# A pooled-attention and gated-convolution kernel: fourteen held output pairs in place of eleven, and another place for the pooling of the next slot's second head pair

## Chip, cores, metric

One core of one Trainium2 chip. The metric is device time in microseconds (us), median over runs. Engines: PE is the matrix engine (PEld its weight loads), DVE the vector engine, ACT the scalar engine, POOL the engine that here issues most DMA transfers, SP one that issues a few. The granted clock is the share of its full clock that PE was given, 1.00 or 0.50 in these traces; 0.50 is called half clock.

## The reference, cut to what matters

```python
# q, k, v: (8, 8, 1152, 64) float32, small values (0.1 * randn)
q_pool = q.reshape(B, H, S // 2, 2, D).mean(axis=3)         # pairs of rows pooled
attn = softmax(q_pool @ k.T / sqrt(D))                      # per head
x = (attn @ v) as (B, S // 2, H * D)                        # (8, 576, 512)
gate = sigmoid(causal_conv5(x, conv_w))                     # per channel
out = ((gate * (x @ w_val)) @ w_out)                        # (8, 576, 512) float32
```

The kernel replaces the softmax by its first-order form, keeps a bound on the error, and computes exactly if the bound fails (it does not here). That part is not touched.

## The kernel before

32 pairs of heads in 16 slots of two (a = 2m, b = 2m + 1). In a slot PE sums k and v (`sm`) and forms the Gram matrices (`g`), ACT evacuates, PE applies them to the transposed pooled q (`xh`), and the convolution (`cps` on PE, three "taps" on DVE), the value matmuls (`vps`) and the gated value (`gv`, DVE) follow. The output matmuls (`ops`) of an earlier batch fill the gaps. Pooling q of the *next* slot (`pool_q`, DVE), its transposes (PE) and their evacuation (`mq`, ACT) are done in the slot before. `warm(n)` issues n idle matmuls (`wps`), whose result nobody reads. `moe` is true once a batch is ready for value and output matmuls (slot 2 on in even slots, slot 3 on in odd ones). Each engine runs its instructions in program order.

```python
NKV = 7            # pairs of inputs in flight
NOSB = 11          # SBUF buffers for finished outputs of two columns
...
def oevac(y, t0, m, ops, eng=None):
    osb = out_pool.tile([128, m, Dm], FP32, name="osb", tag=f"osb{m}", bufs=(3 if m == 1 else NOSB))
    if eng is None:
        nc.scalar.copy(out=osb, in_=ops[:, 0:m])
        held.append((y, t0, m, osb))     # stored only after the last load is issued
        return
    ...
# even slot
    gate(pb)
    gval(bt, 2, val(bt, 2, 0))
    norms(m - 1, g); stat(m, g)
    xhat(a, 1); xhat(b, 2); xevac(a); xevac(b)
    pool_q(a + 2)
    if moe:
        gval(bt, 3, val(bt, 3, 0))
    else:
        warm(3)
    transposes(a + 2)
    squares(m, g)
    conv(a, 1); conv(b, 2)
    tap(a, 0)
    pool_q(b + 2)
    tap(a, 1); tap(a, 2)
    if moe:
        ops = big("ops", 0)              # same PSUM bank as val(bt, 3, 0)
        outs(y, 512 * e, 2, ops, [0])
    ...
    transposes(b + 2)
    tap(b, 0)
    ...                                  # second half of outs, oevac
# odd slot
    ...
    if m + 1 < NSLOT:
        pool_q(a + 2)
        pool_q(b + 2)
    ...                                  # outs, oevac
    conv(a, 1); conv(b, 2, full=m + 1 == NSLOT)
    tap(a, 0)
    if m + 1 < NSLOT:
        transposes(a + 2)
    gate(pb)
    tap(a, 1); tap(a, 2)
    gval(bt, 0, val(bt, 0, 0))
    if m + 1 < NSLOT:
        transposes(b + 2)
    gate(a)
    gval(bt, 1, val(bt, 1, 1))
    if m + 1 < NSLOT:
        tap(b, 0)
    squares(m, g)
    if not moe:
        warm(22)                         # slot 1: idle matmuls
# end of each slot
while nload < min(NPAIR, a + NKV + 1):
    load_pair(nload); nload += 1
if nload == NPAIR:                       # from slot 12 on
    while held:
        store(*held.pop(0), nc.gpsimd)   # the same queue as the loads
```

## Time and profile before

| | before |
|---|---|
| time, median of three runs | 189.31 us (189.28 to 191.28) |
| the profiled run | 190.92 us, span 189.1 |
| PE, DVE, ACT busy | 162.4, 127.3, 111.0 us |
| loads running | to about 148 us (last issue at 136.75, and 11.3 to land) |
| slot 2 starts; slot 14 starts | 42.40; 154.33 us |

The span is the time from the first to the last instruction; the device time is some 1.8 us more. A slot's start, here and below, is its first `sm` matmul in the timeline. The profiled run is one of the longer ones. Besides the half clock at 32.1 to 38.9 us and at 151.6 to 155.0, it has one at 8.2 to 15.0 and one at the end. The views that carry the argument are in the prediction.

### The profile page before, as it was taken

The page shows a single profiled execution, that of the slowest core. Times are in us where ns is not written, and L with a number is a line of the kernel's source. Part 1 is how long each engine was busy: PE and PEld are TensorE (multiplying, and loading weights), DVE is VectorE, ACT ScalarE, POOL GpSimd, SP SyncE. Part 2 cuts the span into 40 slices and gives each one's busy share as a digit, 9 for nine tenths or more (in the row PEclk, how much of TensorE's full clock was granted, in tenths as well). Part 3 has the DMA queues.
Part 4 walks back from the last instruction along what each step waited for, and adds up shares of the span by engine and source line. Part 5 has one row for each costly group of instructions (what it writes and reads, how often), then busy time and mean ns, then how long its engine had stood idle before and what let it go on. Part 6 is the DMA issues. An engine that isn't in the chain of part 4 may idle for free.

```text
span 189.1 us, 5375 instructions
## 1 busy us (share of the span) xinstructions
PE 162.4 (86%) x2269; PEld 113.5 (60%) x2287; DVE 127.3 (67%) x236; ACT 111.0 (59%) x183; POOL 77.2 (41%) x122
## 2 busy tenths in 40 slices
PE   7367893899999999999999999999999599997920
PEld 2155562448678766876686767676867377665500
DVE  3216742906879895989798869888987547956550
ACT  2133952503869586877778686859687365865120
POOL 7945324544454454544344544454543351001000
PEclk9859998589999999999999999999999969999996
DMA  5999999999999999999999999999999999522061
GB/s 195 271 207 207 205 208 206 207 207 208 206 208 206 207 208 206 207 208 207 207 207 207 207 207 207 206 208 207 210 204 235 404 417 413 236 111 114 0 253 38
DMA packets 27864, 40.11 MB, mean 212 GB/s; under 512 B 1909, under 2 KB 24757, under 8 KB 27834
## 3 DMA queue, kind: packets, MB, share of 16 engines
q0 software_dynamic: 26624, 36.61, 97.9%
q1 hardware_dynamic: 938, 2.50, 3.8%
q10 hardware_dynamic: 272, 0.59, 0.9%
q8 instruction: 20, 0.33, 0.6%
q14 instruction: 10, 0.08, 0.1%
HBM read 58.73 MB, written 9.44 MB: 360 GB/s over the span
## 4 chain that ended last, share of the span: by engine, by line
PE 38%; DVE 28%; DMA 19%; ACT 4%; issue 3%; POOL 3%; DVEq 0%; POOLq 0%; ACTq 0%
PE ops L357 11%; DVE acc L318 9%; DVE gv L349 8%; PE vps L341 8%; DMA qn<-in_q_dram 7%; DVE acc L313 7%; DMA out_dram<-osb 6%; DMA kv<-in_k_dram 5%; PE sm L219 5%; PE g L229 4%; PE wps L414 3%; PE cps L303 2%; PE qt_ps L207 2%; PE xh L280 2%; DVE qp L198 2%
## 5 line engine op out<-in xcount | busy, mean ns | idle before, releaser
L318 DVE SCALAR_TENSOR_TENSOR acc<-x,convw_sb,acc 128x576 f32<-128x576 bf16 x62 | 50.5, 814 | 1.4
L341 PE MATMUL vps<-x,wval_sb 128*128 128x288 bf16 x256 | 38.6, 296 | 3.5 <-ACT osb L370 2.2
L357 PE MATMUL ops<-wout_sb,gv 128*128 128x512 bf16 x129 | 35.3, 379 | 0.8
L100 POOL DMA_DIRECT2D kv<-in_k_dram x31 | 22.2, 717 | 30.6 <-DMA kv<-in_v_dram 10.4
L349 DVE TENSOR_TENSOR gv<-vps,gate 128x576 bf16<-128x576 f32 x32 | 24.1, 755 | 12.3 <-PE vps L341 11.5
L313 DVE SCALAR_TENSOR_TENSOR acc<-x,convw_sb,cps 128x576 f32<-128x576 bf16 x31 | 25.1, 809 | 10.8 <-PE cps L303 10.8
L341 PEld LDWEIGHTS <-wval_sb 128*128 128x128 bf16 x256 | 24.5, 100 | 11.7 <-issue 5.0
L209 ACT COPY mq<-qt_ps 128x576 bf16<-128x576 bf16 x32 | 20.5, 639 | 18.4 <-PE qt_ps L207 17.4
L99 POOL DMA_DIRECT2D qn<-in_q_dram x31 | 20.0, 645 | 27.2 <-DVE acc L318 6.5
L287 ACT ACTIVATE x<-xh,stats 128x576 bf16<-128x576 f32 x32 | 22.0, 737 | 7.7 <-DVE stats L259 7.1
L102 POOL DMA_DIRECT2D kv<-in_v_dram x31 | 22.2, 716 | 9.4 <-DMA qn<-in_q_dram 7.0
L325 ACT ACTIVATE gate<-acc 128x576 bf16<-128x576 f32 x31 | 21.3, 686 | 5.3 <-DVE acc L318 5.3
L219 PE MATMUL sm<-kv,first 128*64 128x128 bf16 x576 | 20.4, 227 | 3.7 <-ACT kv L425 3.4
L219 PEld LDWEIGHTS <-first 128*64 128x64 bf16 x576 | 17.8, 114 | 9.2 <-issue 8.3
L265 ACT ACTIVATE mq<-g 64x128 bf16<-64x128 f32 x32 | 8.7, 272 | 23.0 <-PE g L245 22.8
L198 DVE TENSOR_TENSOR qp<-qn 96x768 bf16<-96x768 bf16 x31 | 16.5, 547 | 7.3 <-DMA qn<-in_q_dram 7.3
L370 ACT COPY osb<-ops 128x1024 f32<-128x1024 f32 (+1 forms) x17 | 15.9, 938 | 6.9 <-PE ops L357 4.0
L357 PEld LDWEIGHTS <-gv 128*128 128x128 bf16 x144 | 13.0, 98 | 11.2
L229 PE MATMUL g<-kv 128*64 128x128 bf16 x576 | 19.5, 222 | 0.0
L207 PE MATMUL qt_ps<-ident,qp 96*128 96x96 bf16 x192 | 14.3, 213 | 5.8 <-DVE qp L198 3.8
L364 POOL DMA_DIRECT2D out_dram<-osb x17 | 9.1, 537 | 24.1 <-ACT osb L370 13.6
L303 PE MATMUL cps<-x,diag 128*128 128x288 bf16 x128 | 18.9, 285 | 0.0
(68 smaller groups left out, 157.8 us busy)
## 6 DMA issues: line engine op xcount, KB each, us to landing
qn<-in_q_dram POOLq DMA_DIRECT2D x31, 288.0 KB, 10.9
kv<-in_k_dram POOLq DMA_DIRECT2D x31, 288.0 KB, 10.7
kv<-in_v_dram POOLq DMA_DIRECT2D x31, 288.0 KB, 11.3
out_dram<-osb POOLq DMA_DIRECT2D x14, 512.0 KB, 8.9
out_dram<-osb SPq DMA_DIRECT2D x2, 512.0 KB, 2.9
out_dram<-osb POOLq DMA_DIRECT2D x3, 256.0 KB, 8.2
k<-in_k_dram ACTq DMA_DIRECT2D x1, 576.0 KB, 4.8
q<-in_q_dram SPq DMA_DIRECT2D x2, 288.0 KB, 4.3
```

The lines of the kernel that those rows point to most:

```text
L100: nc.gpsimd.dma_start(out=t[:, W:2 * W].rearrange("p (h x) -> p h x", h=2), in_=k[b, h0:h0 + 2].rearrange("h (p t) d -> p h (t d)", p=128))
L102: nc.gpsimd.dma_start(out=t[:, 0:W].rearrange("p (h x) -> p h x", h=2), in_=v[b, h0:h0 + 2].rearrange("h (p t) d -> p h (t d)", p=128))
L219: nc.tensor.matmul(out=sms[m][64 * h:64 * h + 64, i], lhsT=first, rhs=kvv[:, :, h, t, :], start=(i == 0 and t == 0), stop=(t == NT - 1), s ...
L229: nc.tensor.matmul(out=gs[m][64 * h:64 * h + 64, 128 * i:128 * i + 128].rearrange("p (c d) -> p c d", c=2), lhsT=kvv[:, 1, h, t, :], rhs=k ...
L287: nc.scalar.activation(out=x[:, PAD:].rearrange("p (c n) -> p c n", c=2), in_=xhs.pop(n)[:, :, 0:HALF], func=AF.Identity, bias=stats[:, m, ...
L303: nc.tensor.matmul(out=cps[:, half, 0:HALF], lhsT=w, rhs=x[:, c0:c0 + HALF], start=(i == 0), stop=(i == len(mats) - 1))
L313: nc.vector.scalar_tensor_tensor(out=acc.rearrange("p (c n) -> p c n", c=2), in0=x[:, kk:kk + Sq].rearrange("p (c n) -> p c n", c=2), scal ...
L318: nc.vector.scalar_tensor_tensor(out=accs[n], in0=x[:, kk:kk + Sq], scalar=convw_sb[:, ft, kk:kk + 1], in1=accs[n], op0=ALU.mult, op1=ALU.add)
L325: nc.scalar.activation(out=gt, in_=accs.pop(n), func=AF.Sigmoid)
L341: nc.tensor.matmul(out=vps[:, half, 0:HALF], lhsT=wval_sb[:, fi, ft * 128:(ft + 1) * 128], rhs=x[:, c0:c0 + HALF], start=(fi == 0), stop=( ...
L349: nc.vector.tensor_tensor(out=gvs[y, ft][:, e * Sq:(e + 1) * Sq].rearrange("p (c n) -> p c n", c=2), in0=vps[:, :, 0:HALF], in1=gates.pop( ...
L357: nc.tensor.matmul(out=ops[:, c, :], lhsT=gvs[y, ft][:, t0 + c:t0 + 128 * m:m], rhs=wout_sb[:, ft, :], start=(ft == 0), stop=(ft == NFT - 1))
```

## The change

Its intent: hold all outputs until the loads are issued, so that none waits for a store; and move the pooling of the second pair to places where DVE would wait anyway, or where a late q holds nothing. The core of the diff:

```diff
-    NOSB = 11
+    NOSB = 14
 # even slot
             pool_q(a + 2)
+            transposes(a + 2)
             if moe:
-                gval(bt, 3, val(bt, 3, 0))
+                v3 = val(bt, 3, 0)
+                pool_q(b + 2)
+                gval(bt, 3, v3)
             else:
                 warm(3)
-            transposes(a + 2)
             squares(m, g)
             conv(a, 1)
             conv(b, 2)
             tap(a, 0)
-            pool_q(b + 2)
+            if not moe:
+                pool_q(b + 2)
 # odd slot
             if m + 1 < NSLOT:
                 pool_q(a + 2)
-                pool_q(b + 2)
 ...
             tap(a, 0)
             if m + 1 < NSLOT:
                 transposes(a + 2)
+                if m > 1:
+                    pool_q(b + 2)
 ...
-            if m + 1 < NSLOT:
+            if 1 < m < NSLOT - 1:
                 transposes(b + 2)
 ...
-            if not moe:
-                warm(22)
+            if m == 1:
+                warm(12)
+                pool_q(b + 2)
+                transposes(b + 2)
```

The last hunk is not in the change's title: in slot 1 the second pair's pooling goes to the very end of the slot, and ten idle matmuls go.

## The prediction

> **What bounds the kernel now.** I read the page's slices first, then the chain of work that ended last, then the timeline around each place where the chain is not plain compute. The program runs 16 slots of two head pairs; slot m starts with the 36 `sm` matmuls. The page:
>
> ```profile
> PE 162.4 (86%) x2269; PEld 113.5 (60%) x2287; DVE 127.3 (67%) x236; ACT 111.0 (59%) x183; POOL 77.2 (41%) x122
> PEclk9859998589999999999999999999999969999996
> DMA  5999999999999999999999999999999999522061
> ```
>
> DMA is full for 34 of 40 slices, so a load-bound kernel is the first suspicion. The chain says otherwise. It rests on a transfer in two places only:
>
> ```profile
> 18.57 13.95 DMA qn<-in_q_dram
> ...
> 37.05 5.42 PE wps L414 x20
> ...
> 138.47 11.10 DMA out_dram<-osb
> 149.65 1.02 ACT osb L370
> ```
>
> Up to 32.5 us the start waits for q of pair 5; then 20 idle warm-up matmuls (wps) stand on the path; from 42 to 138 all links are DVE and PE; at 138 to 150 an output copy waits for a store. Busy time by engine in the slots of the steady part (m = 8 to 14, cut at each slot's first `sm`; columns are length, then PE, PEld, DVE, ACT, POOL) says how tight the compute is:
>
> ```profile
> 96.08:105.07 8.99, 8.67 (x138) 6.34 (x138) 8.06 (x14) 6.66 (x12) 4.14 (x6) 1.00 1.19 207
> 105.07:114.45 9.38, 9.33 (x142) 6.84 (x143) 6.87 (x12) 7.19 (x12) 4.23 (x7) 1.00 1.19 207
> ...
> 141.36:154.33 12.97, 10.76 (x142) 7.47 (x142) 7.32 (x12) 8.03 (x14) 5.34 (x10) 0.89 1.10 339
> ```
>
> A slot takes about 9.0 us, PE is busy for nearly all of it and DVE for most. POOL issues a q load every 4.3 us (timeline: 125.51, 129.81, 134.14), so two pairs arrive per 8.65 us: loads are a little faster than compute, and compute falls behind them slowly. Slot 13 is 3.6 us too long.
>
> **What the Trainium skill says.** (1) "DMA: Bandwidth & Descriptors", section Queues, rings and completion order: an engine consumes its ring in order. The trace agrees: the first store, issued by POOL at 138.47 behind eight or so loads, lands 11.1 us later, while the last stores, on the SP queue, take 2.9 us. (2) "TensorE: Matmul & The Clock Gate", Part 1: an idle window of about 3.4 us halves the clock, a busy one restores it. The trace agrees: granted clock 0.50 from 32.1 to 38.9 us, after PE sat idle 2.9 us for q, and 0.50 from 151.6 to 155.0 after the store stall. (3) Same page, section on the array's architecture: ACT and DVE are strict FIFOs, so a held first instruction holds what follows. The trace agrees: PE waits 2.15 us at 150.71 behind the held ACT copy. (4) "VectorE: DVE Perf Modes", the perf-mode tier table: bf16 tensor_tensor runs at 2x. Pooling 768 columns takes 0.55 us, as 768/2 cycles plus the table's fixed part would.
>
> **Part 1: fourteen held output pairs.** Two-column outputs are held in SBUF until the last load is issued at the end of slot 12; by then eleven are held. Slot 13 makes the twelfth, which needs the first store landed:
>
> ```profile
> ACT osb L370 <- DMA out_dram<-osb: 2.9, 1, 2.9
> ```
>
> With fourteen buffers, slots 13 to 15 get free ones, and the last two outputs (fifteenth and sixteenth) reuse buffers whose stores are long done. What it returns is not 11.1 us of store but the excess of slot 13: 12.97 against 9.38 for slot 9, which does the same work: **3.6 us**, with the half-clock window 151.6 to 155.0 in it. Slot 14 (9.29) is no longer than slot 10 (9.26), so no more comes from there. Store traffic stays: about 14 x 1.25 us plus small ones after the last load at about 148 ends near 165, ten us before the final outputs.
>
> **Part 2: slot 1.** Before, DVE stands at q of pair 5 ahead of all taps and gated values:
>
> ```profile
> 32.54 0.56 DVE L198 TENSOR_TENSOR qp<-qn 96x768 bf16<-96x768 bf16 x1 [3.73 <-DMA qn<-in_q_dram]
> 33.02 0.80 DVE L313 SCALAR_TENSOR_TENSOR acc<-x,convw_sb,cps 128x576 f32<-128x576 bf16 x1
> 42.40 1.20 PE L219 MATMUL sm<-kv,first 128*64 128x128 bf16 x36
> ```
>
> After, slot 1 pools only pair 4 first (28.26, when its q lands), so DVE runs three taps from 28.85 to 31.35 (0.81 and two times 0.83), two gated values to 32.8, one tap to 33.6, then pools pair 5 to 34.15, q having landed at 32.5. PE does its eight `vps` at 29.14 and the next eight at 30.3, waits for the first gated value at 32.1, and runs 12 warm matmuls, not 22. In the idle window 28.7 to 32.1 it is now busy some 2.5 us, not 1.42, so I take the clock to stay full: 12 x 0.27 = 3.25, to 35.4. Six transposes (0.4) and the ACT copy out of the bank that `sm` needs (0.64 plus some 0.1) give `sm` of slot 2 at **36.55** in place of 42.40: **5.85 us**. v of pair 5 must be there: q5 at 32.5 plus two transfers of 1.44 gives 35.4 (estimate from the issue pace), a little over in this trace perhaps, but inside 36.5. Later slots: 9 us each against 8.65 of loads, so loads stay ahead, with a smaller margin (about 1 us at slot 2, growing).
>
> **Part 3: the order in even slots** (m = 2 to 14, seven). The chain in slot 8:
>
> ```profile
> 100.46 0.54 DVE L198 TENSOR_TENSOR qp<-qn 96x768 bf16<-96x768 bf16 x1
> 100.51 1.15 PE L341 MATMUL vps<-x,wval_sb 128*128 128x288 bf16 x8 [0.18 <-DVE gv L349]
> 101.76 0.76 DVE L349 TENSOR_TENSOR gv<-vps,gate 128x576 bf16<-128x576 f32 x1 [0.76 <-PE vps L341]
> 103.25 0.55 DVE L198 TENSOR_TENSOR qp<-qn 96x768 bf16<-96x768 bf16 x1
> 103.85 0.43 PE L207 MATMUL qt_ps<-ident,qp 96*128 96x96 bf16 x6
> ```
>
> Before: `vps` at 100.51, gated value, tap, second pooling, transposes at 103.85, four `ops` from 104.12, next `sm` at 105.07. After: the first pair's transposes stand ahead of `vps`, so PE waits for the pooling to end at 101.00: transposes 101.05, `vps` 101.32 (+0.81), convolutions 102.31, four `ops` 103.30, second transposes 104.17 (ready long since), `ops` 104.44, next `sm` about 105.38. DVE saves 0.35 by pooling in the idle 0.76, but PE loses more ahead of `vps` than it recovers at the second transposes: **+0.31 us per even slot**, 2.2 in all.
>
> **Part 4: the order in odd slots** (m = 3 to 13, six). Before, both poolings stand where DVE waits for the convolution anyway (0.76 us idle after them, 1.7 in every other odd slot). After, one stands behind the first tap, in a stretch where DVE has no idle time through the next slot's `gv`. Two dependent taps start 0.85 apart (129.31, 130.16), with a pooling between them 1.20 (102.52, 103.72). So **+0.35 us**, 2.1 in all. In slots 3 and on q has landed in either place.
>
> **The sum.** 189.3 - 3.6 - 5.85 + 2.2 + 2.1 = **184.2 us**, 2.7% less.
>
> **Rivals.** (a) *Loads become the bound*: the earlier start runs into v and q, and the late pooling in odd slots is there because of it. For it: DMA full, margin 1 us at slot 2. Against it: 8.65 a slot against 9.0 or more, and the last load lands near 148, when slot 15 would start at about 159. Then the start's gain is held but not lengthened: a wait of 0.5 to 1.5 us in slots 2 to 4, 185 to 186. (b) *The order costs nothing*: if something in the slots I count as tight has slack, parts 3 and 4 vanish: 179.9. Against it: PE busy 8.67 of 8.99 and DVE back to back in the chain. Half of it would be 182. (c) *The clock drops in slot 1 all the same*: 12 warm matmuls at up to 0.58 each, with the recovery after 3.4 us, add 2 to 3 us: 186.5 to 187. Against it: PE is busier in that window; for it: the window's phase is free. (d) *The reordering costs more*, 0.8 to 1.0 per two slots by the full 0.47 start-to-start of a pooling: 185.
>
> **Range and chances.** The two gains are read from single waits and I trust 3.6 within 0.5; the start within 2.5, mostly downward; the order cost of 4.3 could be anything from 0 to 6. So 181.2 to 187.0. The 2% mark is 185.5, 1.3 above my figure; (a) and (c) and (d) lie on its other side, (b) far on this side: 0.76 faster, 0.22 within, 0.02 slower.
>
> **What would show each step right or wrong.** Right: no output copy waits for a store, and slot 13 takes what slot 9 takes; no half clock after 150; `sm` of slot 2 at 36 to 37 with the clock full from 32; the DVE idle time of q pooling falls from 7.3 us to about 2 or 3; PE idle before the first transposes of each even slot some 0.8 us, two slots taking some 18.8 in place of 18.1. Wrong: slots 2 to 5 waiting for q, k or v (loads bound), half clock at 32 to 39, slots no longer than before (order free), or a wait for a store elsewhere.

## The result and the profile after

184.17 us, median of four runs (184.13 to 184.79), beside 189.5 for the kernel before (189.28 to 191.28). Ratio 0.9706, 95% interval 0.9644 to 0.9769. Ratios here are the mean time of one kernel's runs over that of the other's of the same rounds, so not quite the ratio of the medians quoted. Executions over 1.5% slower than the fastest of the same kernel are left out of the means.

The slices of the page after (PE, DVE, ACT busy time first, then granted clock and DMA share in tenths):

```profile
PE 158.2 (87%) x2277; PEld 111.5 (61%) x2277; DVE 126.0 (69%) x236; ACT 110.9 (61%) x183; POOL 77.3 (42%) x122
PEclk9957999999999999999999999999999999999985
DMA  5999999999999999999999999999999999994070
```

The work is the same; the half-clock slices at 28 to 43 us and near 152 us are gone. DMA is now full to within four slices of the end.

The start and the stall, in the chain of the kernel after:

```profile
14.35 13.73 DMA qn<-in_q_dram
...
31.81 2.75 PE wps L414 x12
34.56 0.27 PE qt_ps L207 x6
34.86 0.65 ACT mq L209
35.55 1.20 PE sm L219 x36
```

Slot 2 starts at 35.55, not 42.40, by the path that the prediction laid out (q of pair 4, taps, gated value, twelve idle matmuls, transposes, ACT copy). No transfer follows in the chain to its end at 182.4: no output copy waits for a store. The slots (busy time by engine, columns as in the prediction; slot 8, slot 9 and slot 13):

```profile
90.89:100.40 9.51, 8.73 (x140) 6.34 (x140) 8.29 (x14) 6.73 (x12) 4.68 (x7) 1.00 1.19 207
100.40:109.78 9.38, 9.38 (x145) 6.83 (x144) 6.43 (x12) 6.95 (x11) 4.13 (x6) 1.00 1.19 206
137.68:147.06 9.38, 9.38 (x143) 6.83 (x142) 6.43 (x12) 6.95 (x11) 3.34 (x7) 1.00 1.18 228
```

Slot 13 takes what slot 9 takes. Slot 8 takes 9.51 us where it took 8.99: PE has the same 8.7 us of work and idles more. Where, the timeline of PE in slot 8 shows:

```profile
95.99 0.43 PE L207 MATMUL qt_ps<-ident,qp 96*128 96x96 bf16 x6 [0.73 <-DVE qp L198]
96.25 1.15 PE L341 MATMUL vps<-x,wval_sb 128*128 128x288 bf16 x8
97.24 1.15 PE L303 MATMUL cps<-x,diag 128*128 128x288 bf16 x8
98.32 1.02 PE L357 MATMUL ops<-wout_sb,gv 128*128 128x512 bf16 x4
```

PE stands 0.73 us at the first pair's transposes, because their pooling is not done; before, it went to `vps` after 0.18. The lengths of all slots from 2 to 14, from the two timelines:

| slot | 2 | 3 | 4 | 5 | 6 | 7 | 8 | 9 | 10 | 11 | 12 | 13 | 14 |
|---|---|---|---|---|---|---|---|---|---|---|---|---|---|
| before | 9.00 | 8.65 | 9.00 | 9.38 | 9.00 | 8.65 | 9.00 | 9.38 | 9.26 | 8.65 | 9.00 | 12.97 | 9.29 |
| after | 9.40 | 8.65 | 9.51 | 9.38 | 9.74 | 8.65 | 9.51 | 9.38 | 9.74 | 8.65 | 9.51 | 9.38 | 9.74 |

Odd slots other than 13 are unchanged, even ones 0.4 to 0.74 longer: 67.15 us in seven in place of 63.55. So between the two profiles 6.85 us came from the start (35.55 and 42.40) and 3.59 from slot 13, and 3.60 went back in even slots: 6.84 in all, beside 6.7 between the spans (189.1 and 182.4); the rest is the tail and rounding.

### The profile page after: what moved, and what is told of

Its sections match the earlier page's. It is cut to its first block, busy times and chain, and to the rows that moved or that the text cites. A ratio compares the mean times of both kernels' runs of the same rounds, so it can differ in the third digit from the quotient of the medians.

```text
span 182.4 us, 5370 instructions
## 1 busy us (share of the span) xinstructions
PE 158.2 (87%) x2277; PEld 111.5 (61%) x2277; DVE 126.0 (69%) x236; ACT 110.9 (61%) x183; POOL 77.3 (42%) x122
## 4 chain that ended last, share of the span: by engine, by line
PE 57%; DVE 20%; DMA 13%; issue 4%; ACT 1%; POOL 1%; DVEq 0%; POOLq 0%
PE ops L357 18%; DMA qn<-in_q_dram 13%; PE vps L341 10%; DVE acc L318 6%; PE cps L303 6%; PE sm L219 6%; DVE acc L313 5%; PE g L229 5%; PE xh L280 4%; DVE qp L198 3%; PE qt_ps L207 3%; DVE gv L349 3%; PE g L254 2%; PE g L243 2%; PE wps L414 2%
## 5 line engine op out<-in xcount | busy, mean ns | idle before, releaser
L341 PE MATMUL vps<-x,wval_sb 128*128 128x288 bf16 x256 | 36.4, 286 | 0.0
L357 PE MATMUL ops<-wout_sb,gv 128*128 128x512 bf16 x144 | 36.0, 379 | 0.0
L349 DVE TENSOR_TENSOR gv<-vps,gate 128x576 bf16<-128x576 f32 x32 | 23.5, 754 | 9.9 <-ACT mq L209 7.2
L341 PEld LDWEIGHTS <-wval_sb 128*128 128x128 bf16 x256 | 23.3, 97 | 5.8
L229 PE MATMUL g<-kv 128*64 128x128 bf16 x576 | 20.0, 225 | 0.0
L207 PE MATMUL qt_ps<-ident,qp 96*128 96x96 bf16 x192 | 13.8, 208 | 6.4 <-DVE qp L198 5.1
L207 PEld LDWEIGHTS <-qp 96*128 96x128 bf16 x192 | 10.9, 98 | 12.9 <-DVE qp L198 8.8
L271 ACT ACTIVATE sq<-mq 128x1152 bf16<-128x1152 bf16 x16 | 18.7, 1167 | 0.0
```

Source lines behind the costliest of these rows:

```text
L207: nc.tensor.transpose(out=qtv[:, u, :], in_=qp[:, u].rearrange("p h d -> p (h d)"), identity=ident[0:QP, 0:QP])
L229: nc.tensor.matmul(out=gs[m][64 * h:64 * h + 64, 128 * i:128 * i + 128].rearrange("p (c d) -> p c d", c=2), lhsT=kvv[:, 1, h, t, :], rhs=k ...
L341: nc.tensor.matmul(out=vps[:, half, 0:HALF], lhsT=wval_sb[:, fi, ft * 128:(ft + 1) * 128], rhs=x[:, c0:c0 + HALF], start=(fi == 0), stop=( ...
L349: nc.vector.tensor_tensor(out=gvs[y, ft][:, e * Sq:(e + 1) * Sq].rearrange("p (c n) -> p c n", c=2), in0=vps[:, :, 0:HALF], in1=gates.pop( ...
L357: nc.tensor.matmul(out=ops[:, c, :], lhsT=gvs[y, ft][:, t0 + c:t0 + 128 * m:m], rhs=wout_sb[:, ft, :], start=(ft == 0), stop=(ft == NFT - 1))
```

## Experiments

Eleven runs, all with correct results. "Before" beside each is the kernel before in the same rounds on the same chip; its median moves from job to job (189.6 to 191.0), so the ratios decide.

### Each gain alone: 14 pairs, the start, and one without the other

```diff
# e1: the kernel before
-    NOSB = 11
+    NOSB = 14
```

> The kernel before with 14 held pairs and nothing else. My theory: the wait of the twelfth output copy for the first store goes, slot 13 takes 9.4 us in place of 12.97. The profiled run of before was one of its longer ones (190.92 us) and held a half-clock window after the stall, so 190.9 - 3.6 = 187.3 us; that is 2.1 below the median of before. Rival: the 11.1 us of store in the chain are the path, and more than 3.6 us come back (under 185). Other rival: the time comes back as another wait in slots 14 and 15 (189).

Measured: 187.23 us (before 189.62), ratio 0.9884 (0.9821 to 0.9948). In its profile slot 13 takes 9.38 us and no output copy waits for a store. As expected, and neither rival: not the 11.1 us of the chain, and the time does not come back as another wait.

```diff
# e2: the changed kernel
-    NOSB = 14
+    NOSB = 11
```

> The changed kernel with 11 held pairs as before. My theory: the landing of the first store, near 149.6 us, hangs on the loads and not on compute, so the earlier start only lengthens the wait: the twelfth copy is ready at about 143.3, waits 6.3 us, slot 14 starts near 154 as in the kernel before, and the end is 189 to 191 us: the whole gain of the start is lost. Rival, the parts simply add: 184.2 + 3.6 = 187.8 us or less.

Measured: 191.68 us (before 189.62), ratio 1.0083 (1.0024 to 1.0143), a little over the 189 to 191 us expected. Slot 2 starts at 35.54 as in the changed kernel, and slot 14 at 154.92, where the kernel before has 154.33. The whole of the start is gone, in the ACT wait (total, times, longest, from the waits of ACT in slot 13):

```profile
ACT osb L370 <- DMA out_dram<-osb: 6.5, 1, 6.5
```

6.5 us where the kernel before waits 2.9. The parts do not add.

The cleaner form, the start alone in the old order, came last:

```diff
# e11: the kernel before
             if m + 1 < NSLOT:
                 pool_q(a + 2)
-                pool_q(b + 2)
+                if m > 1:
+                    pool_q(b + 2)
 ...
-            if m + 1 < NSLOT:
+            if 1 < m < NSLOT - 1:
                 transposes(b + 2)
 ...
-            if not moe:
-                warm(22)
+            if m == 1:
+                warm(12)
+                pool_q(b + 2)
+                transposes(b + 2)
```

> The kernel before with the change of slot 1 and nothing else (11 held pairs, old order in all later slots). My theory, after two more profiles of the kernel before in which slot 2 started 1 to 1.5 us sooner and slot 14 no sooner: with 11 pairs the end hangs on the landing of the first store, near 149.6 us, so slot 2 starts at 35.5 and slot 14 still starts at 153 to 155.5; 188.5 to 191 us, no gain. Rival, a gain of the start that is kept whatever the stores do: 182.5 to 184.

Measured: 191.52 us (before 191.03), ratio 1.0051 (1.0002 to 1.01); a little outside what I expected, on the worse side. Slot 2 starts at 36.32, slot 13 at 135.29 (before: 141.36), and slot 14 at 154.12. The ACT wait, and the chain across it:

```profile
ACT osb L370 <- DMA out_dram<-osb: 8.7, 1, 8.7
```

```profile
138.62 10.69 DMA out_dram<-osb
...
149.39 1.02 ACT osb L370
```

The six us that slot 2 gains are six us more of waiting: 8.7 less 2.9. PE is idle longer too, and gets a half-clock window of 6.8 us (146.4 to 153.3) where the profile of before had one of 3.4.

Two more profiles of the kernel before say the same without any edit.

> The kernel before, unchanged, profiled once more. Its runs spread over 3 us and its profile was of a long one (190.92 us, span 189.1), with a half-clock window after the store stall. My theory: in a shorter run (span 187.1 to 187.7) that window is absent or elsewhere, slot 13 takes about 11.4 us, not 12.97, and the stall costs 2.0 us, as the kernel with 14 pairs alone gained 2.4. Rival: the spread is in the start, before slot 2, and slot 13 takes 12.9 us in every run.

> The same kernel a second time, since the phase of the clock's windows cannot be chosen: one of the two should show the other state. Same numbers as for the first.

Measured: 191.02 and 192.01 us, single runs of unknown state. Neither the theory nor the rival came true, and both runs were long ones again: slot 13 took 14.99 and 15.12 us, longer than in the first profile, not shorter. What happened says more than what I expected: with half clock in other places (one early window, 10.8 to 21.1 or 8.0 to 21.6, and none at 32 to 39) slot 2 started at 40.85 and 41.37, 1.0 to 1.5 us sooner than in the first profile, and slot 14 at 154.81 and 155.46, no sooner. In the chains of the two, the copy comes right after the store; here is the first, and in the second the store runs 10.67 us from 139.86 and the copy starts at 150.61:

```profile
139.11 10.70 DMA out_dram<-osb
149.89 1.02 ACT osb L370
```

In five profiles with 11 pairs, with slot 2 at 35.5 to 42.4, the twelfth copy starts at 149.4 to 150.6. That is the anchor: in all five the store is issued at 138.3 to 139.9, behind the last loads on the same queue, and takes 10.7 to 11.2 us, whatever slot 2 did. Why most runs of before are at 189 and some at 191, I did not catch: all three profiles are of runs of 191 to 192 us and have a half-clock window right after the stall. That the shorter runs lack it is possible (their mean granted clock is mostly higher, 0.951 to 0.962 in those of span 187.1 to 187.2) but not shown, and the evidence is weak: e9 has 0.952 at a span of 189.3, and a run of span 187.4 has 0.940.

### The order, undone by halves

```diff
# e3: the changed kernel, even slots
             pool_q(a + 2)
-            transposes(a + 2)
             if moe:
-                v3 = val(bt, 3, 0)
-                pool_q(b + 2)
-                gval(bt, 3, v3)
+                gval(bt, 3, val(bt, 3, 0))
             else:
                 warm(3)
+            transposes(a + 2)
 ...
             tap(a, 0)
-            if not moe:
-                pool_q(b + 2)
+            pool_q(b + 2)
```

> The changed kernel with the old order in even slots. My theory: the new order costs 0.31 us in each of seven even slots, because PE waits for the first pooling ahead of vps; undone, 184.2 - 2.2 = 182.0 us, and PE idles 0.2 us there, not 0.7. Rival: the new order saves DVE time that the next slots would need, or keeps q waits away: 184.5 to 186 us.

Measured: 181.5 us (before 189.62), ratio 0.9566 (0.9519 to 0.9614), 2.7 us under the changed kernel. Even slots take 9.11 or 9.35 in place of 9.51 or 9.74: 0.4 less each. No wait for q appears after slot 1.

```diff
# e4: the changed kernel, odd slots
             if m + 1 < NSLOT:
                 pool_q(a + 2)
+                if m > 1:
+                    pool_q(b + 2)
 ...
                 transposes(a + 2)
-                if m > 1:
-                    pool_q(b + 2)
```

> The changed kernel with the old order in odd slots 3 to 13 (both poolings ahead of the outputs). My theory: the pooling behind the tap costs the following even slot 0.2 to 0.35 us, six times: 182.1 to 183.0 us, with no wait for q in slot 3 or later. Rival: since slots start earlier now, q of the second pair comes late in odd slots and holds the taps, which is what the new place is for: 185 us or more, with DVE waiting for q in slots 3, 5 and 7.

Measured: 183.91 us (before 189.62), ratio 0.9689 (0.9645 to 0.9733): 0.3 us under the changed kernel by the medians, not told from it by the intervals. I had expected 182.1 to 183.0. In the profile the step is larger than in the medians: even slots take 9.40, one 9.67, in all 1.1 us less than in the changed kernel, as expected, and the span is 181.3 beside 182.4. But the profiled run is among the shorter of the six (the others span 181.6 to 182.5). Their mean granted clock is a little lower (0.959 to 0.968; the changed kernel 0.966 to 0.979); that this took the rest back is not shown. DVE waits 0.3 us for q in slot 3, once; slot 3 still takes 8.65.

```diff
# e5: both edits of e3 and e4
```

> The changed kernel with the old order in even slots and in odd slots 3 to 13; slot 1 and the 14 held pairs stay. My theory: nothing of the new order is needed, so the two undone costs add: 181.5 (even slots undone) less some 1.2 (odd slots undone: even slots 9.12 and 9.35 become 9.0) gives 180.3 us. Rival: now that the slots are shorter, compute catches up with the loads in slots 3 to 7 and the late q holds the taps: no better than 181.5, with DVE waiting for q by over 1 us in all after slot 2.

Measured: 180.49 us (before 190.8), ratio 0.9498 (0.9438 to 0.9558). Slots are those of the kernel before to 0.01 us in nearly every case (9.00, 8.65, 9.00, 9.38), slot 13 too is 9.38. The rival has a grain of truth. The waits of DVE from 44 us on:

```profile
DVE qp L198 <- DMA qn<-in_q_dram: 1.0, 2, 0.7
```

In slots 3 and 5 q of the second pair comes 0.65 and 0.33 us late, which is what the new place in odd slots is safe from. But it costs nothing: those slots take 8.65 and 9.38, since DVE would wait for the convolution after it anyway. So e5 is the kernel before with 14 pairs and the change of slot 1, and nothing else of the change is needed.

One even slot (12), in e3, e4, e5 and then the changed kernel (busy time by engine):

```profile
126.03:135.14 9.11, 8.80 (x139) 6.34 (x138) 8.28 (x14) 6.84 (x12) 4.18 (x7) 1.00 1.19 207
```

```profile
127.59:136.99 9.40, 8.67 (x140) 6.34 (x140) 8.08 (x14) 6.55 (x12) 4.62 (x8) 1.00 1.19 207
```

```profile
125.60:134.60 9.00, 8.73 (x139) 6.34 (x139) 8.07 (x14) 6.67 (x12) 4.49 (x7) 1.00 1.19 207
```

```profile
128.17:137.68 9.51, 8.74 (x139) 6.34 (x138) 8.29 (x14) 6.74 (x12) 4.80 (x8) 1.00 1.19 207
```

The even order alone adds 0.40 here, the odd order alone 0.11, the two 0.51. The odd order's share differs by slot: with the old even order (e3 less e5) it is 0.11 us in slots 4, 8 and 12, whose odd slot before has four `ops` behind the poolings, and 0.34, 0.08 and 0.34 in slots 6, 10 and 14, whose odd slot before has eight: 1.1 in all. With the new even order (changed kernel less e4) the profiles give the same to 0.02 us.

### A better order

```diff
# e6: e5, with this in even slots
             pool_q(a + 2)
             if moe:
-                gval(bt, 3, val(bt, 3, 0))
+                v3 = val(bt, 3, 0)
+                pool_q(b + 2)
+                gval(bt, 3, v3)
             else:
                 warm(3)
             transposes(a + 2)
 ...
             tap(a, 0)
-            pool_q(b + 2)
+            if not moe:
+                pool_q(b + 2)
```

> As the last, but in even slots the second pair is pooled ahead of the gated value as in the change, while the first pair's transposes stay behind the value matmuls as in the kernel before. My theory: the idle DVE time takes the pooling, PE loses nothing ahead of vps, and the 0.25 us that PE idled at the second transposes go: even slots of 8.75 us, seven times, 178.5 us. Rival: q of pair 7 in slot 2 or the loads hold it (over 180).

Measured: 179.58 us (before 190.8), ratio 0.9413 (0.9357 to 0.9469): faster than both kernels, and than e5 by the medians (the intervals overlap). It is 1.1 us over what I expected, though the slots came as expected. The timeline of slot 12 (PE and DVE):

```profile
129.84 1.01 DVE L198 TENSOR_TENSOR qp<-qn 96x768 bf16<-96x768 bf16 x2
129.89 1.15 PE L341 MATMUL vps<-x,wval_sb 128*128 128x288 bf16 x8 [0.18 <-DVE gv L349]
131.14 0.76 DVE L349 TENSOR_TENSOR gv<-vps,gate 128x576 bf16<-128x576 f32 x1 [0.29 <-PE vps L341]
```

`vps` starts 0.18 after PE's last work, as before, and both poolings fit where DVE waited 0.76 for it; 0.29 of that is left. Even slots take 8.74 in six of seven (slot 10: 9.01). Its profiled run, 180.24, was the longest of six, with half clock from 10.7 to 21.0 and slot 2 only at 36.78 (35.62 in e5, with half clock from 11.0 to 14.5). Why the other runs are over 178.5 too was not looked into.

### The idle matmuls of slot 1

```diff
# e7: the changed kernel
-                warm(12)
+                warm(22)
# e8: the changed kernel
-                warm(12)
```

> The changed kernel with 22 warm matmuls in slot 1 as before, not 12. My theory: they stand on the path at 0.21 to 0.27 us each, so slot 2 starts 2.1 to 2.7 us later: 186.3 to 186.9 us. Rival: slot 2 starts with v of pair 5, not with PE, and the warm matmuls are hidden: 184.2.

> The changed kernel without any warm matmuls in slot 1. My theory: the last value of pair 5 lands near 35.6 us and slot 2 started at 35.55, so the second pair's sums are held by the load: little or nothing gained (183.5 to 184.2 us) if the clock stays full, and a loss of 1 to 2 us if PE's idle time of about 2 us in slot 1 makes a half-clock window. Rival: the warm matmuls are the bound of slot 2's start and the start comes 1 us or more sooner: 183.2 or less.

Measured: e7 186.91 us (before 190.8), ratio 0.9821 (0.9743 to 0.9899), slot 2 at 37.73 in place of 35.55: ten matmuls are 2.2 us of path, and all of it arrives (0.9821 less 0.9706 of 190 us is 2.2). e8 184.87 us, ratio 0.97 (0.9622 to 0.9777): no better than the changed kernel (0.9706). Its slot 2 starts at 34.95, 0.6 sooner, and then takes 10.99 us, because the clock drops. The stretches 28.7 to 32.1, 32.1 to 35.5 and 35.5 to 38.9 of e8 (first column after the length is PE busy; PEclk is the third from the right):

```profile
28.70:32.10 3.40, 2.47 (x23) 1.73 (x22) 3.33 (x6) 2.08 (x5) 1.35 (x3) 1.00 1.20 207
32.10:35.50 3.40, 0.98 (x24) 0.94 (x25) 1.64 (x3) 1.68 (x2) 1.86 (x3) 1.00 1.19 208
35.50:38.90 3.40, 3.40 (x68) 3.16 (x64) 1.97 (x3) 0.00 (x0) 1.56 (x3) 0.50 1.20 206
```

PE was busy 0.98 of 3.4 us, and the next stretch ran at half clock. With the twelve idle matmuls the changed kernel has 2.72 and 2.68 us busy in its own stretches of 3.41 us there (30.01 to 33.42 and 33.42 to 36.83: its clock changes at 16.35 us, and these lie whole stretches later), and keeps the full clock. So in these two profiles the twelve pay for themselves; whether six would do was not tried, and a run without them whose windows lie elsewhere was not profiled.

## Why the prediction came out as it did

**The time** was predicted at 184.2 and measured at 184.17. The direction of every term held, the cause too except in part 4, and no rival came true. The sizes of the terms were off by 0.5 to 1.2 us each; that they cancelled to 0.03 is luck. Three small readings were off as well: DMA is at 9 tenths in 33 slices, not 34; DVE's idle time for q fell to 3.9 us, not 2 or 3; and two slots take 18.6 us on average, not 18.8.

- *Part 1, the store stall, 3.6 us.* The mechanism held: nothing waits for a store any more, slot 13 takes what slot 9 takes. The size held between the profiles (3.59). Alone it is worth 2.4 us of median (e1), because I read it from a run that was 1.6 us longer than the median I subtracted it from.
- *Part 2, slot 1, 5.85 us.* Slot 2 moved by 6.85 us in the profiles. The steps held (first taps at 28.58, idle matmuls end at 34.4); the idle matmuls went at 0.22 us each (31.81 to 34.40), where I took 0.27 from a stretch partly at half clock; that is 0.6 of the 1.0 us, and the earlier taps most of the rest. With 14 pairs in both, the part is worth 187.23 - 180.49 = 6.7 us (medians of e1 and e5, in two jobs; by the ratios, 0.9884 less 0.9498, some 7.3; by slot 2 in the two profiles, 42.31 and 35.62, 6.7).
- *What the prediction did not say*: the two are not separate gains. With 11 pairs the end hangs on the first store, and the start is worth nothing (e11, e2, the two repeated profiles). Ratios to the kernel before, in the old order: 14 pairs alone 0.9884, the start alone 1.0051, both 0.9498. My sum came out because both were in the change.
- *Part 3, even slots, +0.31 each, 2.2 in all.* Right in kind and place: PE waits ahead of `vps`. Measured 0.40 each and 2.7 us (e3). The term that I missed is 0.09: `ops` uses the PSUM bank that the gated value reads, and in the timeline of slot 8 that value runs from 97.51 to 98.27 and `ops` start at 98.32, where 97.24 and the usual 0.99 would make 98.23. In e4, which has the even order alone, slot 12 shows the same 0.09 (134.91 beside 133.83 + 0.99).
- *Part 4, odd slots, +0.35 each, 2.1 in all.* The sign held, the size did not: by the slots of the profiles 1.1 us, with either even order; by the medians 0.3 beside the new one (e4) and 1.0 beside the old (e3 to e5). The step that failed is the tightness: I took a stretch of DVE as tight because no idle time was listed. A pooling there does cost DVE more, but in e3 (slot 11) the two gated values behind it take 1.41 us and not 1.55, as waits too short to be listed went, and in slot 12 only 0.11 of 0.35 reaches PE. Slots 6 and 14 do lengthen by 0.34; why slot 10 does so by only 0.08 was not looked into.
- *The rivals.* (a) Loads as the bound: waits for q of 0.3 to 0.65 us do appear (0.5 in slot 2 of the changed kernel), and none lengthens a slot. (b) The order is not free. (c) The clock stayed full; e8 shows how near it was. (d) The order cost 3.7 us in all (184.17 - 180.49), not more than 4.3.
- *What it took from the Trainium skill.* Points (1) and (2) fit, with two limits: the page states (1) where it treats the queues of SP and ACT, and says there that completion need not be in order, so the 11.1 us rest on the trace; and the idle time before half clock was shorter than the page's window (see the last section). For (3) the line given does not show the order of ACT: `vps` at 150.71 waits for the copy itself, which empties its PSUM bank. What shows it is the next ACT instruction: the `mq` copy, whose transposes ended at 148.56, starts at 150.56, right behind the held copy. Point (4) is an estimate: the tier table has no fixed part, but its row, 1224 ns for 2048 columns, leaves some 0.16 us beside 1024 cycles at the page's 0.96 GHz, and so 0.56 us for 768 columns, beside 0.55 measured.

In sum: -2.4 for the stall alone, -6.7 for the start once the stall is gone, +1.0 and +2.7 for the odd and the even order make -5.4, and 189.6 - 5.4 = 184.2. These are the steps from before over e1, e5 and e3 to the changed kernel, so they add up by construction; medians of different jobs can shift each of them.

## What to carry to other kernels

Before adding up gains, ask which event the end hangs on: a wait for a transfer that runs on its own clock swallows every earlier gain, so the buffer that removes it and the gain ahead of it are worth little alone and much together. When one edit bundles several moves, undo them one at a time: here two of four were losses hidden under the gain of the others, and the kernel with only the right half of one of them (e6) is the fastest. To move work of one engine into a time when it waits for another is free only if the same edit does not make the other wait for that work: the second pooling fitted DVE's wait for `vps`, and what cost 0.40 us was to put the first pair's transposes ahead of `vps`.

## What the Trainium skill lacked or had wrong

- "TensorE: Matmul & The Clock Gate", section HAM oscillation, gives the rule as no PE-idle gaps over about 3.4 us. Here shorter gaps sufficed: a stretch of 3.4 us with PE busy 1.42 us and its idle gap 2.86 us long (before, 28.7 to 32.1), one with 1.26 us and 2.15 us (before, 147.3 to 150.7), and one with 0.98 us and 2.54 us (e8), were each followed by half clock; stretches with 2.72 and 2.68 us busy (after) and one with 1.85 us busy and a gap of 1.26 us (e9, 31.4 to 34.8) were not. How much of a window must be busy is on no page; whether the share or the gap decides, these runs do not tell.
- The same page's statement that the window runs freely agrees: three profiles of the kernel before have their half clock before slot 2 at 8.2 to 15.0 and 32.1 to 38.9 us in one, and at 10.8 to 21.1 or 8.0 to 21.6 in the others, and slot 2 starts up to 1.5 us sooner in these. The page speaks of this for the first matmuls of a kernel; that a half-clock stretch in mid-kernel can come or go with it, as the one at 32.1 does, it does not say.
- "DMA: Bandwidth & Descriptors" gives a first-byte latency of about 1 us and a fixed cost of about 2 us; no page has the time of a transfer that joins a full software queue. Here it is 10.7 to 11.3 us at the median for 288 KB loads and 10.7 to 11.2 us for the first store, and 2.9 us for a store of the same 512 KB on SP's queue at the end, with no loads running. These runs do not separate the kind of queue from the backlog.
- "VectorE: DVE Perf Modes", section The DRAIN you can't avoid, says that an instruction that is not held may start earlier, without a figure. Here two dependent taps start 0.85 us apart, a pooling starts 0.73 us after a tap of 0.81, and a pooling of 0.55 between two dependent taps costs 0.35.
